# Moving the token differences of two of the four difference products of the w_out matmul from GpSimd to VectorE, with new contention constants in the ordering

## The chip, the cores and the metric

The kernel runs on one core of one Trainium2 chip. The metric is the device time of one execution in microseconds (us), lower is better; several runs are given by their median.

## What is computed

Attention in chunks of 64 tokens, then a relu-squared feed-forward layer, then a gated feed-forward layer, all in float32 (the reference, cut):

```python
scores = scale * np.matmul(q_c, k_c.transpose(0, 1, 2, 4, 3))   # 8 batches, 8 heads, 9 chunks of 64, head size 64
attn = softmax(scores)
x = (attn @ v_c) as tokens                   # 4608 tokens x 512
h = np.maximum(x @ w_in, 0.0)                # w_in 512 x 2048
y = h * h @ w_out                            # w_out 2048 x 512
gate = 1.0 / (1.0 + np.exp(-(y @ w_gate)))   # w_gate, w_val 512 x 1536
out = gate * (y @ w_val) @ w_out2            # w_out2 1536 x 512
```

## The kernel before, in words

All features lie on the 128 partitions, tokens on the free axis. Every large matmul is made by a Strassen-like scheme: the two operands are cut in 2 x 2 blocks, and seven products P1 to P7 take the place of eight. Four of them (P5, P6, P7, P4) take a difference of two token blocks as their moving operand, the other three (P1, P2, P3) a block as it is. Every operand is split in two fp32r parts, high and low: ScalarE rounds it (line 428), VectorE subtracts the rounded part from it (`split`, line 433), and TensorE adds up three fp32r matmuls for each (high x high, low x high, high x low).

The w_out product is made by class `Long` (from line 898), one object for each of six pairs of token blocks of 384 tokens. The inner size of 2048 is 16 blocks of 128: eight for each half, so each product has eight groups (index `kp`) of six matmuls of 128x384 (two output halves by three terms, line 934). `long_units` (line 986) gives the products' order on TensorE: P1 of this pair, P4 of the last pair, then P2, P5, P6, P3, P7 of this pair. `blocks_g` (line 1097) loads the blocks g of h*h from DRAM with a look of 13 us; b11, b12 and b22 are loaded once in a pair, b21 twice. `Long.product` calls `minus` (line 905) ahead of the four difference products, and `minus` issues eight subtractions of 128x384 through `binary` (line 439), here on GpSimd for all four: 4 x 8 x 6 = 192 in this stage. They are made in place: P5 turns b11 into b12 - b11, P6 turns that into b22 less it, P7 turns b12 into b22 - b12, P4 subtracts from the second b21 what P6 left. Then `split(x, r, n, look=5.0)` (line 927) makes the operand; the `look` of 5.0 lets the planner take its buffer at most 5 us before the split is due. The last stage (the gated layer's w_out2) uses `Long` too, with blocks of 512.

The order of all instructions on all engines comes from a planner (class `Plan`, from line 52). Each piece of work is a job with an engine, a planned cost and the buffers that it reads and writes. `due` (line 89) works backward from TensorE's order to a due time for each job; `run` (line 119) simulates all engines and lets each engine take, when it is free, the ready job with the earliest due time that its memory allows. Costs come from `cost` (line 397), as fixed part plus part per element, and jobs marked `shared` (VectorE's and GpSimd's work with all operands in SBUF) are lengthened when the other engine is at a shared job (lines 203 to 206). The times of this simulation set only the order; on the chip each engine runs its list and waits on semaphores. The weights of the gated layer are prepared beside the w_out stage (`weight_group`, line 526, buffers `wf`, `ws`, `wx`): conversions on ScalarE and VectorE, an integer addition and four sums on GpSimd, splits, and a DMA to DRAM.

Of the kernel before, what the change touches and what calls it, by code (L numbers as in the profile page):

```python
# [14 lines left out]
ALU = mybir.AluOpType  # L15
# [36 lines left out]
class Plan:  # L52
# [66 lines left out]
    def run(self):  # L119
# [4 lines left out]
        engines = {e: 0.0 for e in ("PE", "ACT", "DVE", "POOL", "SP")}  # L124
# [9 lines left out]
                heapq.heappush(ready[j.eng], (j.due, j.n))  # L134
        events, order = [], []
        t, dma, shift, done = 0.0, 0.0, 0.0, 0
        port = {"DVE": 0.0, "POOL": 0.0}
        stall, why = 0.0, {}

        def place(b):  # L140
# [50 lines left out]
        def begin(j):  # L191
            nonlocal dma, done, shift
            j.start, j.started = t, True
            done += 1
            order.append(j)
            if j.eng == "SP":
                engines["SP"] = t + j.cost
                dma = max(dma, t) + j.bytes / 270e3
                j.end = max(dma, t + j.cost) + self.DMA_LATENCY
            else:  # L200

                cost = j.cost
                if j.shared:
                    other = "POOL" if j.eng == "DVE" else "DVE"
                    cost += min(cost, max(0.0, port[other] - t)) * (1.0 if j.eng == "DVE" else 0.4)
                    port[j.eng] = t + cost
                engines[j.eng] = t + cost
                j.end = t + cost + (0.35 if j.eng == "PE" else 0.15)
            heapq.heappush(events, (engines[j.eng], ~j.n))
            heapq.heappush(events, (j.end, j.n))  # L210
# [3 lines left out]
        while done < len(jobs):  # L214
            moved = True
            while moved:
                moved = False
                for e in engines:
# [23 lines left out]
                    while ready[e] and tries < 600:  # L242
                        due, n = heapq.heappop(ready[e])
                        j = jobs[n]
# [31 lines left out]
            t, n = heapq.heappop(events)  # L276
# [3 lines left out]
            for n in batch:  # L280

                j = jobs[n if n >= 0 else ~n]
# [41 lines left out]
def tile_attention_relu2_glu(  # L324
# [24 lines left out]
    BL1 = 384  # L349
# [45 lines left out]
        return Buf(psum=True, name=name)  # L395

    def cost(eng, n, flat=None):
        per = {"ACT": (0.17, 0.0009), "DVE": (0.1, 0.00115), "POOL": (0.2, 0.0022)}[eng]
        return per[0] + per[1] * n


# [37 lines left out]
    def binary(eng, o, a, b, op, n, ob, ib, soon=None, look=None):  # L439
        e = {"DVE": nc.vector, "POOL": nc.gpsimd}[eng]  # L440
        return job(
            eng, cost(eng, n), lambda: e.tensor_tensor(out=o(), in0=a(), in1=b(), op=op),  # L442
            [*ib], [*ob], soon=soon, look=look, shared=not any(x.psum for x in ib),
        )
# [165 lines left out]
    def product(ps, ops, xs, p, n, first, cost_of, at_=None):  # L610
        kind, half = A_OF[p]
        op, x = ops[kind], xs[B_OF[p]]
        size = op.size // 8
        reads = [op, *x]

        def go():
            o = at(ps, n)
            for kk in range(2):
                if len(x) == 2:
                    xb, off, xsize = x[kk], 0, n  # L620
                else:
                    xb, off, xsize = x[0], kk * n, 2 * n
                for i, (wi, xi) in enumerate(((0, 0), (1, 0), (0, 1))):
                    nc.tensor.matmul(  # L624
                        out=o,
                        lhsT=at(op, P, F32R, wi * size + half * HB + kk * P),
                        rhs=at(xb, n, F32R, xi * xsize + off),
                        start=(first and kk == 0 and i == 0),
                        stop=(kk == 1 and i == 2),
                        skip_group_check=True,  # L630
                    )

        return job("PE", 6 * cost_of, go, reads if first else [*reads, ps], [ps], stream="main", at=at_)
# [208 lines left out]
    class Unit:  # L842
        def __init__(self, ops, xs, n, per, finish, tag):
            self.ops, self.xs, self.n, self.per, self.finish, self.tag = ops, xs, n, per, finish, tag
# [51 lines left out]


    class Long:
        def __init__(self, ops, blocks, n, per, finish):
            self.ops, self.blocks, self.n, self.per, self.finish = ops, blocks, n, per, finish  # L900

        def words(self, b):
            return lambda: at(b, self.n)

        def minus(self, o, x, y):
            for oo, xx, yy in zip(o, x, y):
                binary("POOL", self.words(oo), self.words(xx), self.words(yy), ALU.subtract,
                       self.n, [oo], {oo, xx, yy})

        def product(self, ps, p, first):  # L910
            n = self.n
            need = {"P1": "11", "P2": "21", "P5": "11 12", "P6": "11 22", "P3": "22", "P7": "12 22", "P4": "11 21"}[p]
            have = {x: self.blocks((int(x[0]) - 1, int(x[1]) - 1)) for x in need.split()}
            b11, b12, b21, b22 = (have.get(x) for x in ("11", "12", "21", "22"))
            src = {"P1": b11, "P2": b21, "P5": b11, "P6": b11, "P3": b22, "P7": b12, "P4": b21}[p]
            if p == "P5":
                self.minus(b11, b12, b11)
            elif p == "P6":
                self.minus(b11, b22, b11)
            elif p == "P7":  # L920
                self.minus(b12, b22, b12)
            elif p == "P4":
                self.minus(b21, b21, b11)
            kind, half = A_OF[p]
            for kp, r in enumerate(src):
                x = Buf(8 * n, name="x", op=True)
                split(x, r, n, look=5.0)
                w = self.ops[kp][kind]

                def go(kp=kp, x=x, w=w):  # L930
                    size = w.size // 8
                    for m in range(2):
                        for i, (wi, xi) in enumerate(((0, 0), (1, 0), (0, 1))):
                            nc.tensor.matmul(  # L934
                                out=at(ps[m], n),
                                lhsT=at(w, P, F32R, wi * size + half * HB + m * P),
                                rhs=at(x, n, F32R, xi * n),
                                start=(first and kp == 0 and i == 0),
                                stop=(kp == len(src) - 1 and i == 2),
                                skip_group_check=True,  # L940
                            )

                new = first and kp == 0
                job("PE", 6 * self.per, go, [w, x] if new else [w, x, *ps], ps, stream="main")
# [65 lines left out]
    with tc.manual_schedule():  # L1010

        per1, per, per_h = 0.1735, 0.227, 0.1195
        pairs1 = NT // (2 * BL1)
# [83 lines left out]
        def blocks_g(s):  # L1097
            def load(r, c):
                got = []
                for kp in range(G1):  # L1100
                    t = sbuf(BL1, "g")
                    f, b = r * G1 + kp, 2 * s + c
                    dma(lambda t=t: at(t), lambda f=f, b=b: gd[f][:, b * BL1:(b + 1) * BL1],
                        [gb[f, b]], [t], size=P * BL1 * 4, look=13.0)
                    got.append(t)
                return got

            return block_loader(load)

        def finish_y(s):  # L1110
            def finish(u, m, col, t):
                a = (2 * s + col) * BL1
                d = yb[m, 2 * s + col] = Buf(name="yd")
                dma(lambda: yd[:, m, a:a + BL1], lambda: at(t), [t], [d], size=P * BL1 * 4, soon=3.0)
            return finish

        def y_of(m, a, n):
            return [yb[m, b] for b in range(a // BL1, (a + n - 1) // BL1 + 1)]

        w1out = [weight_group(None, f, G1, f"wo{f}", True, look=55.0, raws=raws1, by=rows, have=w1f) for f in range(G1)]  # L1120
        long_units([
            (lambda s=s: Long(w1out, blocks_g(s), BL1, per1, finish_y(s))) for s in range(pairs1)
        ])


# [92 lines left out]
        def finish3(s):  # L1218
            def finish(u, m, col, t):
                n = u.n  # L1220
                o = sbuf(n, "o")
                job("DVE", 0.1 + 0.00118 * n, lambda: nc.vector.transpose(out=at(o), in_=at(t)), [t], [o], soon=2.0)
                t0 = s[col] * BLK if len(s) == 2 else col * HB

                def dst():
                    return [out[t0:t0 + n, m * P + 32 * g:m * P + 32 * g + 32].rearrange(
                        "(b t) c -> t b c", t=32) for g in range(4)]

                def src():
                    return [at(o)[32 * g:32 * g + 32].rearrange("p (b c) -> p b c", c=32) for g in range(4)]  # L1230

                dma(dst, src, [o], size=P * n * 8, n=4, soon=2.0)
            return finish

        long_units([
            (lambda s=s: Long(wo, last_blocks(s), BLK if len(s) == 2 else HB,
                              per if len(s) == 2 else per_h, finish3(s)))
            for s in order[1]
        ])

# [31 lines left out]
```

## Time and profile before

| | |
|---|---|
| median of 3 runs | 1705.0 us (1704.69 to 1706.76) |
| profiled execution | 1700.49 us |
| its span, first to last instruction | 1698.7 us |
| mean granted TensorE clock | 0.990 |
| busy: TensorE, VectorE, ScalarE, GpSimd | 1632.5, 1419.0, 985.7, 953.9 us |
| stages by the trace: start-up; attention and w_in; w_out; gate and value; w_out2 | to 150; 520.5; 895.5; 1431.6; 1698.7 us |

In the profile PE is TensorE's matmuls, PEld its weight loads, DVE VectorE, ACT ScalarE, POOL GpSimd, SP the queue that issues the DMAs. Times are us from the span's start. A busy time counts each instruction from its start to its end; overlapping instructions of TensorE are counted once. L934 is line 934 of the kernel. The share of busy time is an average over stages; what bounds a stage is read from that stage.

### The profile page before, as it was taken

What the parts mean: (1) busy time and instruction counts of PE and PEld (TensorE: products, weight loads), DVE (VectorE), ACT (ScalarE), POOL (GpSimd) and SP (SyncE); (2) the same over time, 40 slices, a digit from 0 to 9 for tenths busy, and PEclk for the clock granted to TensorE, in tenths of its full rate; (3) what the DMA queues carried; (4) which work ended last, traced back from release to release, by engine and by line L of the source; (5) the groups of instructions that cost most, each with busy time, mean ns of one, the idle gap of its engine ahead of it and who ended that gap; (6) DMA issues with size and microseconds to landing.
All of it is one profiled execution on the core that took longest, in us unless ns stands there. A gap on an engine that the chain in (4) does not pass through costs nothing. (4 is left out here: it accounts for less than half of the span.)

```text
span 1698.7 us, 30837 instructions
## 1 busy us (share of the span) xinstructions
PE 1632.5 (96%) x10452; PEld 1453.1 (86%) x10452; DVE 1419.0 (84%) x1928; ACT 985.7 (58%) x1974; POOL 953.9 (56%) x740
## 2 busy tenths in 40 slices
PE   6789999999999999999999999999999999999998
PEld 5678999899999998999988879878887789788888
DVE  7998686768789999999999988764678855999996
ACT  7676565666676555655556656544545644455554
POOL 2653021211358678768687777653656745777662
PEclk8999999999999999999999999999999999999999
DMA  9925657676686644854885853687365478666662
GB/s 246 217 80 156 160 139 197 175 207 180 206 285 203 199 164 131 276 177 131 270 301 171 289 182 137 223 286 259 131 217 217 158 274 300 194 166 162 169 169 50
DMA packets 390798, 333.35 MB, mean 196 GB/s; under 512 B 234736, under 2 KB 325616, under 8 KB 390640
## 3 DMA queue, kind: packets, MB, share of 16 engines
q1 hardware_dynamic: 390640, 331.38, 63.0%
q8 instruction: 82, 1.34, 0.3%
q14 instruction: 76, 0.62, 0.1%
HBM read 209.13 MB, written 122.16 MB: 195 GB/s over the span
## 5 line engine op out<-in xcount | busy, mean ns | idle before, releaser
L498 POOL TENSOR_TENSOR wf__2712<-wf__2712,wr__2649 128x512 int32<-128x512 int32 x16 | 20.9, 1305 | 229.5 <-DVE wf__2712 L491 131.1
L442 POOL TENSOR_TENSOR raw__537<-raw__696,raw__537 128x384 f32<-128x384 f32 x24 | 30.0, 1268 | 41.7 <-DVE B__730 L433 24.7
L498 POOL TENSOR_TENSOR wf__6803<-wf__6803,wr__6481 128x512 int32<-128x512 int32 x18 | 26.9, 1495 | 45.7 <-DVE wf__6803 L491 36.6
L498 POOL TENSOR_TENSOR wf__7393<-wf__7393,wr__6481 128x512 int32<-128x512 int32 x18 | 25.1, 1397 | 38.8 <-DVE wf__7393 L491 19.5
L479 ACT ACTIVATE wr__6481<-wr__6481 128x512 int32<-128x512 uint32 x36 | 23.9, 664 | 0.0
L433 DVE TENSOR_TENSOR wx__8063<-ws__7534,wx__8063 128x512 fp32r<-128x512 f32 x18 | 20.5, 1141 | 1.3 <-ACT wx__8063 L428 1.3
L475 ACT ACTIVATE wf__6803<-wr__6481 128x512 f32<-128x512 f32 x18 | 12.0, 664 | 15.2 <-DVE wx__8063 L433 8.3
L482 DVE TENSOR_SCALAR wf__7393<-wf__7393 128x512 f32<-128x512 f32 x18 | 13.2, 731 | 8.6 <-ACT wf__7393 L475 8.6
L433 DVE TENSOR_TENSOR wx__7334<-ws__7534,wx__7334 128x512 fp32r<-128x512 f32 x18 | 16.4, 912 | 3.7 <-ACT wx__7334 L428 3.7
L442 DVE TENSOR_TENSOR b__10264<-b__10264,bank 128x512 f32<-128x512 f32 x7 | 4.8, 688 | 16.8 <-PE bank L624 12.1
L482 DVE TENSOR_SCALAR wf__6803<-wf__6803 128x512 f32<-128x512 f32 x18 | 11.8, 656 | 7.7 <-ACT wf__6803 L475 7.7
L498 POOL TENSOR_TENSOR w__669<-w__669,wraw__374 128x512 int32<-128x512 int32 x1 | 1.3, 1289 | 29.7 <-DVE w__669 L491 29.7
L442 DVE TENSOR_TENSOR b__10691<-b__10691,bank 128x512 f32<-128x512 f32 x7 | 4.8, 686 | 15.2 <-PE bank L624 13.3
L442 POOL TENSOR_TENSOR ws__7534<-wf__6803,wf__7393 128x256 f32<-128x256 f32 x18 | 17.1, 952 | 0.5
L442 POOL TENSOR_TENSOR ws__7534<-ws__7534,wf__6803 128x256 f32<-128x256 f32 x18 | 16.7, 926 | 1.0
L433 DVE TENSOR_TENSOR wx__7443<-wf__7393,wx__7443 128x256 fp32r<-128x256 f32 x18 | 15.2, 842 | 1.6 <-ACT wx__7443 L428 1.6
L491 DVE SCALAR_TENSOR_TENSOR wf__7393<-wr__6481,wf__7393 128x512 int32<-128x512 int32 x18 | 16.1, 894 | 0.3
L491 DVE SCALAR_TENSOR_TENSOR wf__6803<-wr__6481,wf__6803 128x512 int32<-128x512 int32 x18 | 15.6, 866 | 0.3
L484 DVE TENSOR_SCALAR wf__7393<-wf__7393 128x512 int32<-128x512 int32 x18 | 15.2, 843 | 0.6
L442 POOL TENSOR_TENSOR raw__696<-raw__696 128x384 f32<-128x384 f32 x12 | 14.8, 1249 | 0.0
L475 ACT ACTIVATE wf__7393<-wr__6481 128x512 f32<-128x512 f32 x18 | 11.9, 664 | 4.6 <-DMA wr__6481<-in_moe_w_val_dram 2.2
L442 POOL TENSOR_TENSOR raw__537<-raw__537 128x384 f32<-128x384 f32 x12 | 14.5, 1226 | 0.0
(5638 smaller groups left out, 6671.8 us busy)
## 6 DMA issues: line engine op xcount, KB each, us to landing
ad<-wx__7334 SPq DMA_DIRECT2D x27, 512.0 KB, 4.5
ad<-wx__8063 SPq DMA_DIRECT2D x27, 512.0 KB, 4.2
wr__2649<-in_moe_w_out_dram SPq DMA_DIRECT2D x16, 512.0 KB, 4.5
wr__6481<-in_moe_w_gate_dram SPq DMA_DIRECT2D x12, 512.0 KB, 4.5
wr__6481<-in_moe_w_val_dram SPq DMA_DIRECT2D x12, 512.0 KB, 4.2
wr__6481<-in_moe_w_out_dram SPq DMA_DIRECT2D x12, 512.0 KB, 3.9
ad<-wx__7443 SPq DMA_DIRECT2D x18, 256.0 KB, 3.7
wf<-wf__2712 SPq DMA_DIRECT2D x16, 256.0 KB, 4.7
```

What stands on the lines that cost most here:

```text
L433: lambda: nc.vector.tensor_tensor(out=lo(), in0=at(src, n, F32, off), in1=hi().bitcast(F32), op=ALU.subtract),
L442: eng, cost(eng, n), lambda: e.tensor_tensor(out=o(), in0=a(), in1=b(), op=op),
L475: nc.scalar.activation(out=at(w), in_=t[:, :, 1].bitcast(F32), func=ACTF.Abs)
L479: nc.scalar.activation(out=low, in_=low.bitcast(U32), func=ACTF.Copy, scale=2.0**-29)
L482: nc.vector.tensor_scalar_max(at(w), at(w), TINY)
L484: nc.vector.tensor_scalar(out=wi, in0=wi, scalar1=5, scalar2=2, op0=ALU.logical_shift_left, op1=ALU.logical_shift_right,)
L491: nc.vector.scalar_tensor_tensor(out=wi, in0=words()[:, :, 1], scalar=-0x40000000, in1=wi, op0=ALU.bitwise_and, op1=ALU.bitwise_or,)
L498: nc.gpsimd.tensor_tensor(out=wi, in0=wi, in1=words()[:, :, 0], op=ALU.add)
```

## The change

The subtractions of P5 and P6 of the w_out product go to VectorE, those of P7 and P4 stay on GpSimd. The last stage's `Long` gets an empty table, so all four stay on GpSimd there. The planner's cost of a GpSimd instruction becomes 0.3 + 0.0024 n. Its contention rule changes: a VectorE job that starts while GpSimd is at a shared job is lengthened by 0.45 of GpSimd's remaining time, at most 0.82 of its own cost, and by a debt that GpSimd jobs ran up when they started beside a VectorE job; a GpSimd job is lengthened by 0.1 of the overlap instead of 0.4. The rule holds for all stages.

```diff
-        port = {"DVE": 0.0, "POOL": 0.0}
+        port = {"DVE": 0.0, "POOL": 0.0, "debt": 0.0}
...
-                if j.shared:
-                    other = "POOL" if j.eng == "DVE" else "DVE"
-                    cost += min(cost, max(0.0, port[other] - t)) * (1.0 if j.eng == "DVE" else 0.4)
-                    port[j.eng] = t + cost
+                if j.shared and j.eng == "DVE":
+                    cost += port["debt"] + min(0.82 * cost, 0.45 * max(0.0, port["POOL"] - t))
+                    port["debt"], port["DVE"] = 0.0, t + cost
+                elif j.shared:
+                    cost += 0.1 * min(cost, max(0.0, port["DVE"] - t))
+                    port["debt"] += 0.45 * min(cost, max(0.0, port["DVE"] - t))
+                    port["POOL"] = t + cost
...
-        per = {"ACT": (0.17, 0.0009), "DVE": (0.1, 0.00115), "POOL": (0.2, 0.0022)}[eng]
+        per = {"ACT": (0.17, 0.0009), "DVE": (0.1, 0.00115), "POOL": (0.3, 0.0024)}[eng]
...
     class Long:
-        def __init__(self, ops, blocks, n, per, finish):
+        def __init__(self, ops, blocks, n, per, finish, engines):
+            self.engines = engines
...
-        def minus(self, o, x, y):
+        def minus(self, p, o, x, y):
             for oo, xx, yy in zip(o, x, y):
-                binary("POOL", self.words(oo), self.words(xx), self.words(yy), ALU.subtract,
+                binary(self.engines.get(p, "POOL"), self.words(oo), self.words(xx), self.words(yy), ALU.subtract,
                        self.n, [oo], {oo, xx, yy})
...
-            (lambda s=s: Long(w1out, blocks_g(s), BL1, per1, finish_y(s))) for s in range(pairs1)
+            (lambda s=s: Long(w1out, blocks_g(s), BL1, per1, finish_y(s), {"P5": "DVE", "P6": "DVE"})) for s in range(pairs1)
...
-                              per if len(s) == 2 else per_h, finish3(s)))
+                              per if len(s) == 2 else per_h, finish3(s), {}))
```

## Rows read from the trace of the kernel before

**Rows 1.** The page's first part: busy time, share of the span and instructions by engine.

```profile
PE 1632.5 (96%) x10452; PEld 1453.1 (86%) x10452; DVE 1419.0 (84%) x1928; ACT 985.7 (58%) x1974; POOL 953.9 (56%) x740
```

**Rows 2.** Busy time by stage: stretch, its length, each engine's busy us, clock, DMA.

```profile
0.00:150.00 150.00, 117.12 (x1309) 103.30 (x1310) 134.75 (x216) 105.78 (x219) 74.07 (x70) 0.92 0.74 180
150.00:520.50 370.50, 363.22 (x3349) 341.60 (x3348) 284.27 (x518) 238.68 (x524) 89.54 (x80) 1.00 0.68 196
520.50:895.50 375.00, 366.83 (x2019) 348.65 (x2018) 368.62 (x427) 214.64 (x440) 283.00 (x226) 1.00 0.60 198
895.50:1431.60 536.10, 525.02 (x2521) 440.80 (x2520) 384.92 (x494) 293.38 (x550) 331.77 (x249) 0.99 0.63 223
1431.60:1698.70 267.10, 260.32 (x1260) 218.79 (x1259) 246.45 (x277) 133.18 (x244) 175.54 (x119) 1.00 0.57 148
```

**Rows 3.** Line 934 in the w_out stage, then TensorE's timeline at both its ends.

```profile
520.50:895.50 375.00, 366.71 (x2016) 348.31 (x2016) 1.00 0.60 198
...
520.56 1.20 PE L934 MATMUL bank<-x__6303,woa__5763 128*128 128x384 f32 x6
521.60 1.20 PE L934 MATMUL bank<-x__6330,woa__5793 128*128 128x384 f32 x6
...
895.27 0.86 PE L624 MATMUL bank<-B__9769,g__9480 128*128 128x512 f32 x3
```

**Rows 4.** Busy time by products: P2, P5, P6 of each pair; last, the final stretch.

```profile
528.88:556.59 27.71, 27.25 (x146) 24.61 (x145) 27.14 (x27) 16.54 (x37) 23.32 (x19) 1.00 0.25 78
590.13:616.88 26.75, 26.71 (x146) 24.68 (x146) 26.75 (x30) 13.80 (x28) 22.38 (x18) 1.00 0.23 74
651.43:679.70 28.27, 26.59 (x145) 24.73 (x145) 28.27 (x32) 14.21 (x29) 21.34 (x18) 1.00 0.33 105
712.98:740.90 27.92, 27.50 (x145) 24.59 (x145) 27.92 (x30) 15.01 (x31) 23.11 (x19) 1.00 0.31 101
774.18:802.21 28.03, 27.89 (x145) 24.52 (x145) 28.00 (x27) 13.15 (x27) 26.13 (x21) 1.00 0.27 86
835.74:864.63 28.89, 27.52 (x146) 24.47 (x145) 28.86 (x30) 15.13 (x32) 25.72 (x21) 1.00 0.92 318
...
864.63:895.44 30.81, 27.27 (x146) 26.42 (x146) 30.66 (x36) 18.23 (x35) 23.25 (x18) 0.94 0.66 226
```

**Rows 5.** GpSimd's timeline in the second pair: four of a run of 24 differences.

```profile
581.22 1.02 POOL L442 TENSOR_TENSOR g__6342<-g__6424,g__6342 128x384 f32<-128x384 f32 x1 [5.69 <-DMA g__6424<-gd]
...
602.73 1.01 POOL L442 TENSOR_TENSOR g__6247<-g__6396,g__6247 128x384 f32<-128x384 f32 x1
...
608.84 1.32 POOL L442 TENSOR_TENSOR g__6823<-g__6195,g__6823 128x384 f32<-128x384 f32 x1
610.12 1.32 POOL L442 TENSOR_TENSOR g__6842<-g__6220,g__6842 128x384 f32<-128x384 f32 x1
```

**Rows 6.** VectorE's timeline before and during that run: splits (L433), a PSUM addition.

```profile
575.97 0.54 DVE L433 TENSOR_TENSOR x__6399<-g__6301,x__6399 128x384 fp32r<-128x384 f32 x1
576.44 0.54 DVE L433 TENSOR_TENSOR x__6468<-g__6815,x__6468 128x384 fp32r<-128x384 f32 x1
...
588.89 1.37 DVE L433 TENSOR_TENSOR x__6427<-g__6478,x__6427 128x384 fp32r<-128x384 f32 x1
590.19 1.37 DVE L433 TENSOR_TENSOR x__6303<-g__6195,x__6303 128x384 fp32r<-128x384 f32 x1
...
601.80 0.54 DVE L442 TENSOR_TENSOR e__2080<-e__2080,bank 128x384 f32<-128x384 f32 x1
```

**Rows 7.** TensorE at the run's end; its weight loads' largest wait on VectorE.

```profile
605.01 1.44 PE L934 MATMUL bank<-x__6399,wos__6394 128*128 128x384 f32 x6
606.29 1.45 PE L934 MATMUL bank<-x__6468,wos__6476 128*128 128x384 f32 x6
...
PEld bank L934 <- DVE x__6383 L433: 3.3, 9, 0.8
```

**Rows 8.** Line 442 in the w_out stage: VectorE's and GpSimd's busy time and instructions.

```profile
520.50:895.50 375.00, 18.12 (x36) 269.81 (x218) 1.00 0.60 198
```

More of the change, by code (lines that the diff above doesn't have):

```diff
@@ L916, in product @@
             if p == "P5":
-                self.minus(b11, b12, b11)
+                self.minus(p, b11, b12, b11)
             elif p == "P6":
-                self.minus(b11, b22, b11)
+                self.minus(p, b11, b22, b11)
             elif p == "P7":
-                self.minus(b12, b22, b12)
+                self.minus(p, b12, b22, b12)
             elif p == "P4":
-                self.minus(b21, b21, b11)
+                self.minus(p, b21, b21, b11)
             kind, half = A_OF[p]
```

## The prediction

> **What bounds the kernel now.** First the page's busy line [rows 1]: TensorE is busy 96% of the span and VectorE 84%, but these are averages over stages with different limits. So next the busy time by stage [rows 2]. In the w_out stage, from 520.5 to 895.5 us, VectorE is busy 368.62 of 375.00 us (98.3%), GpSimd 283.00, TensorE 366.83. In no other stage do both elementwise engines come so near to full at once.
>
> A busy TensorE is not TensorE at its peak, so I count its pace. Its 2016 matmuls of line 934 are 336 groups of six (one token block each); a free group starts 1.04 us after the one before, the first at 520.56, and the next stage's first matmul follows at 895.27 [rows 3]. At the free pace 336 groups take 336 x 1.04 = 349.4 us; they took 374.7. **The excess is 25.3 us**, and that is the most that this stage can give.
>
> Where it lies: the six stretches of the products P2, P5, P6 (24 groups, 24.96 us free) last 167.6 us together instead of 149.8, so 17.8 us of it is theirs. The last stretch (P3, P7 and P4 of the last pair, also 24 groups) lasts 30.81 instead of 24.96: 5.9 us, at the hand-over to the next stage, where granted clock dips to 0.94 [rows 4]. The remaining products hold 1.7.
>
> Why P5 and P6: GpSimd makes the differences of P5, P6 and P7 of one token pair as one unbroken run of 24, from 581.22 to 611.4 us, one each 1.28 us; the single one that ran beside VectorE's PSUM additions took 1.01 [rows 5]. Beside such a run VectorE makes one split per GpSimd instruction: starts 1.30 us apart, 1.37 long. With GpSimd still, the same split takes 0.54 and the next starts 0.47 later; the PSUM addition keeps 0.54 in the middle of the run [rows 6]. So the two engines go in lockstep at 1.29 us a pair, and **each GpSimd difference costs VectorE 1.29 - 0.47 = 0.82 us**. TensorE wants a split each 1.04 us, so in such a run VectorE loses 0.25 us per group; 24 of them eat 6 us, more than the lead of about 5 us that the splits' look of 5.0 allows. At the end of the run TensorE's groups come 1.28 apart, and its weight loads wait for VectorE's split [rows 7]. Four runs of eight per pair, six pairs: 192 differences, of line 442's 218 on GpSimd [rows 8].
>
> **The change, part by part.** *Removed from GpSimd:* the differences of P5 and P6, 2 x 8 x 6 = 96, at 1.29 us: 124 us of its 283 in this stage. GpSimd is on nobody's path by itself, so this alone gives nothing. What it gives is VectorE's time: 96 x 0.82 = 78.7 us.
>
> *Added to VectorE:* 96 subtractions of 128x384 f32 with both inputs in SBUF. That is the split's own form, so the price lies between 0.47 us (GpSimd still) and 1.29 us (in lockstep) [rows 6]. I take 0.47, since of the unbroken run of 24 only eight stay, and the differences can be made before or after those: 96 x 0.47 = 45.1 us. VectorE's load: 368.6 - 78.7 + 45.1 = 335.0 us, for TensorE's 349.4. At 1.29 each it would be 413.8, and the stage slower; both ends are used below.
>
> By the Trainium skill (SBUF — State Buffer, Who interferes with whom) the shared port pair is an exclusive lock for a whole instruction whenever VectorE has two SBUF inputs and GpSimd reads SBUF; a pair would then take 1.01 + 0.47 = 1.48 us, a difference would cost VectorE 1.01, and the load would fall to 316.8. The trace has 1.29, and it decides; nothing below uses the 1.48.
>
> *What a P5 or P6 product then needs:* a difference and a split per group, 0.94 us on VectorE against TensorE's 1.04. It keeps up, barely. The P7 run of eight that is left costs 8 x 0.25 = 2 us of the lead of 5, and the P4 run the same in another place. So the 17.8 us of P2, P5 and P6 can go nearly to nothing; bounds 0 and 17.8. I leave 2.8 (half a microsecond per pair, for weight work of the GLU stage that falls between): **15 us gained**. The 5.9 at the hand-over stay: there GpSimd turns to the GLU stage's token differences, which are not moved. The 1.7 stay too.
>
> *Waits that move:* each moved difference waits on VectorE for the load of its second block. Behind it on that engine stand the splits, for which TensorE waits. GpSimd waited 5.69 us so at the start of one run, idle and early [rows 5]; an equally late load on VectorE would use up the lead, so its price is 0 to about 1 us per pair. I take 0: that run starts at 581.22 [rows 5], and TensorE reaches its product at 590.13 + 8 x 1.04 = 598.5 at the earliest [rows 4], 17 us later. No DMA is added or removed, no instruction moves to SP, and ScalarE's copies for the splits are the same.
>
> *The planner's constants:* a GpSimd instruction is now planned at 0.3 + 0.0024 n instead of 0.2 + 0.0022 n (1.22 us for 384, nearer to the 1.29 of the trace than 1.04), and the mutual delays are charged otherwise. For a run of eight both versions charge VectorE some 0.6 us per GpSimd instruction, so I expect no drift in one direction. But every stage's order is drawn anew. TensorE's idle time outside this stage is 32.9 us in the first 150 us, and 11.1 and 6.8 in the last two stages [rows 2]; the stage between has 7.3. I take 0 and keep plus and minus 6 us, a tenth of those 58.
>
> **Sum.** The profiled execution took 1700.5 us around a span of 1698.7; minus 15 is 1685.5. The median of the runs shown is 1705.0, 4.5 above it, and all terms are differences, so I forecast 1705 - 15 = **1690 us**. A change of less than 0.2% (3.4 us) can't be told from none here.
>
> **The rivals.** *Same: the stall finds another place.* P6's differences and P7's need the same blocks (b22), so GpSimd's run for P7 starts just when VectorE has P6's to make. Beside that run of 10.3 us VectorE makes eight instructions while TensorE uses up ten groups; if all eight are differences rather than splits, the lead shrinks by 10 us and TensorE stalls 5 us per pair, against 25.3 / 6 = 4.2 now. Against it: VectorE's order goes by due time, and splits that are due first go first; with three or fewer differences among the eight the lead holds (5 us, less the 2 us above, is three groups). Time: about 1704. Chance 0.14.
>
> *Slower: VectorE is the full engine and gets more to do.* GpSimd's freed 124 us are filled with preparation of the GLU weights, whose additions of SBUF words stretch VectorE just as the differences did. VectorE's relief per microsecond of GpSimd work that vanishes is 0.82 / 1.29 = 0.64, so the 45.1 us added are paid for as long as 71 us stay empty: the point is a refill of 53 us, where GpSimd's work other than differences is now 283 - 192 x 1.29 = 35 us in this stage. At 88 us of refill VectorE gets 45.1 - 0.64 x 36 = 22 us more, and the GLU stage, thus relieved, can give back at most its 11.1: some 12 us slower, 1717. For it: VectorE has no idle time to show for [rows 2], and the planner fills what is ready. Against it: weight work has far later due times and needs VectorE itself between its GpSimd steps. Chance 0.12.
> The Trainium skill (Perfetto Trace Analysis, Optimizing Scalar/DVE Operations) points the same way: a saturated VectorE should hand work to ScalarE or even GpSimd; but it adds that between these two it might not help, as they share a port, and the lockstep of this trace agrees with that half.
>
> *Faster still:* the whole 25 goes, since the hand-over also gets an earlier GpSimd: 1680. Chance 0.10. *Lost elsewhere:* the 15 us come, and the new order loses as much in the first 150 us or the GLU stage: 1702 to 1708. Chance 0.06. The forecast has the other 0.58. That the subtraction would not run on VectorE is excluded: the engine is an argument of the call.
>
> **How the numbers follow.** Faster by over 0.2%: 0.58 and 0.10, and 0.04 from the rival of the other place, which may keep a few microseconds: 0.72. Same: the rest of that rival and half of the loss elsewhere: 0.13. Slower: the refill and what is left: 0.15. The forecast's own range is 1683 to 1697 (15 gained, plus or minus 6, and 1 for the wait). With the 25 us case below and the cases near zero above it becomes 1679 to 1707; the refill is left out.
>
> **What would show it.** In the changed trace: the w_out stage in about 360 us; 96 differences on GpSimd, in runs of eight; P5 and P6 groups 1.04 apart; VectorE's subtraction at 0.47 apart outside the runs and 1.29 inside; VectorE's share still above 93%. Wrong if P6's groups still come 1.28 apart, if runs of weight work fill GpSimd to 88 us beside its differences, or if the first 150 us or the GLU stage moves by over 6 us.

## The result and the profile after

The changed kernel takes 1680.82 us (median of four runs, 1678.82 to 1681.26), beside 1705.51 for the kernel before: a ratio of 0.9852, 95% interval 0.9835 to 0.9869. That is 24.7 us faster, where 15 were forecast. The profiled execution took 1678.82 us around a span of 1677.0, 21.7 us less than the span of before.

The page's busy line, the answer to [rows 1]:

```profile
PE 1623.2 (97%) x10452; PEld 1458.9 (87%) x10452; DVE 1397.7 (83%) x2024; ACT 981.9 (59%) x1974; POOL 836.7 (50%) x644
```

96 instructions have gone from GpSimd to VectorE, and yet VectorE's busy time is lower than before (1397.7, was 1419.0). Next the busy time by stage, the answer to [rows 2]; the stages are cut at each stage's first matmul (and at 150 us):

```profile
0.00:150.00 150.00, 116.70 (x1280) 103.36 (x1281) 130.86 (x210) 101.72 (x211) 66.41 (x64) 0.90 0.75 180
150.00:527.05 377.05, 369.37 (x3378) 349.51 (x3377) 287.16 (x523) 240.86 (x529) 91.82 (x82) 0.99 0.67 193
527.05:881.75 354.70, 352.06 (x2017) 349.03 (x2017) 345.82 (x530) 217.11 (x445) 170.80 (x135) 1.00 0.67 221
881.75:1423.20 541.45, 538.22 (x2589) 451.08 (x2589) 398.73 (x501) 298.92 (x561) 341.05 (x252) 1.00 0.62 219
1423.20:1677.00 253.80, 246.87 (x1194) 205.87 (x1192) 235.12 (x265) 123.33 (x231) 166.63 (x113) 1.00 0.56 145
```

The last cut lies 15 us late: the w_out2 stage's first matmul starts at 1407.88. With it the stages are 527.1 (was 520.6), **354.7 (374.7)**, **526.1 (536.1)** and 269.2 us (267.3): 6.5 us lost ahead of the w_out product, 20.0 gained in it, 10.0 gained in the gate and value stage (the GLU stage below), 1.9 lost in the last.

The busy time by products, the answer to [rows 4], P2, P5 and P6 of each pair and then the final stretch:

```profile
535.37:560.88 25.51, 25.49 (x146) 24.84 (x145) 25.51 (x42) 14.40 (x34) 10.14 (x8) 1.00 0.21 73
594.16:619.12 24.96, 24.96 (x146) 24.96 (x145) 24.05 (x37) 14.63 (x30) 11.06 (x9) 1.00 0.33 104
652.40:677.36 24.96, 24.96 (x146) 24.96 (x145) 24.93 (x41) 13.98 (x30) 10.29 (x8) 1.00 0.34 111
710.64:736.68 26.04, 25.49 (x145) 24.89 (x145) 25.46 (x42) 14.87 (x32) 10.10 (x8) 1.00 0.32 109
769.96:794.92 24.96, 24.96 (x145) 24.96 (x145) 24.33 (x41) 14.61 (x31) 10.01 (x8) 1.00 0.35 116
828.20:853.38 25.18, 25.18 (x145) 24.94 (x145) 24.77 (x42) 14.18 (x31) 11.93 (x8) 1.00 1.00 366
853.38:881.75 28.37, 26.30 (x145) 24.76 (x145) 28.34 (x33) 17.85 (x35) 23.80 (x18) 1.00 0.84 297
```

At the free pace of 1.04 us a group each row would be 24.96. Three of the six are exactly that; the six sum to 151.6 us, an excess of 1.9 (it was 17.8). GpSimd's busy time in each has gone from over 21 us to between 10 and 12. The final stretch, which is the hand-over to the next stage, has 3.4 us of excess. Before it was 5.7: [rows 4] cuts that stretch at 895.44, but the next stage's first matmul starts at 895.27 [rows 3]. What is left of the stage, 168 groups, takes 174.7 us, which is 168 x 1.04: no excess. The total excess is 5.3 us, was 25.3.

VectorE's timeline in the second pair, the answer to [rows 6]: L446 with g is a moved difference, L437 a split.

```profile
589.37 0.55 DVE L446 TENSOR_TENSOR g__6753<-g__6322,g__6753 128x384 f32<-128x384 f32 x1
589.84 0.55 DVE L446 TENSOR_TENSOR g__6491<-g__7010,g__6491 128x384 f32<-128x384 f32 x1
590.30 0.55 DVE L437 TENSOR_TENSOR x__7053<-g__6160,x__7053 128x384 fp32r<-128x384 f32 x1
...
597.56 1.36 DVE L437 TENSOR_TENSOR x__6305<-g__6737,x__6305 128x384 fp32r<-128x384 f32 x1
598.84 1.37 DVE L437 TENSOR_TENSOR x__7053<-g__6426,x__7053 128x384 fp32r<-128x384 f32 x1
...
608.22 0.55 DVE L446 TENSOR_TENSOR g__6753<-g__6294,g__6753 128x384 f32<-128x384 f32 x1
608.68 0.55 DVE L437 TENSOR_TENSOR x__6975<-g__6426,x__6975 128x384 fp32r<-128x384 f32 x1
```

And GpSimd's run for P7 in between, first and last of eight, the answer to [rows 5]:

```profile
592.61 1.92 POOL L446 TENSOR_TENSOR g__6972<-g__7055,g__6972 128x384 f32<-128x384 f32 x1 [14.24 <-DMA g__7055<-gd]
...
602.34 1.33 POOL L446 TENSOR_TENSOR g__7044<-g__6202,g__7044 128x384 f32<-128x384 f32 x1
```

P5's differences come before the run, and instructions start 0.47 us apart there; only the last two of the eight overlap the run's first difference, and are no longer for it. In the run VectorE makes splits alone, in lockstep at 1.29; P6's differences come after it, alternating with splits, again at 0.47.

Not every pair is so clean. In the last pair, VectorE and then GpSimd:

```profile
834.00 1.37 DVE L437 TENSOR_TENSOR x__7553<-g__6322,x__7553 128x384 fp32r<-128x384 f32 x1
835.29 1.36 DVE L446 TENSOR_TENSOR g__6972<-g__8651,g__6972 128x384 f32<-128x384 f32 x1
836.57 1.37 DVE L437 TENSOR_TENSOR x__9520<-g__6270,x__9520 128x384 fp32r<-128x384 f32 x1
837.87 1.37 DVE L446 TENSOR_TENSOR g__6426<-g__6327,g__6426 128x384 f32<-128x384 f32 x1
```

```profile
832.16 2.79 POOL L446 TENSOR_TENSOR g__6839<-g__7532,g__6839 128x384 f32<-128x384 f32 x1 [8.15 <-DMA g__7532<-gd]
834.91 1.33 POOL L446 TENSOR_TENSOR g__7044<-g__6258,g__7044 128x384 f32<-128x384 f32 x1
```

Here four of the sixteen moved differences go in lockstep with GpSimd's run. In the whole stage it is 12 of 96, at 1.36 to 1.38 us each; the other 84 take 0.54 to 0.56.

### The profile page after: what moved, and what is told of

It reads as the page before. It is cut to its first block, busy times and chain, and to the rows that moved or that the text cites. A ratio compares the mean times of both kernels' runs of the same rounds, so it can differ in the third digit from the quotient of the medians.

```text
span 1677.0 us, 30764 instructions
## 1 busy us (share of the span) xinstructions
PE 1623.2 (97%) x10452; PEld 1458.9 (87%) x10452; DVE 1397.7 (83%) x2024; ACT 981.9 (59%) x1974; POOL 836.7 (50%) x644
## 5 line engine op out<-in xcount | busy, mean ns | idle before, releaser
L446 POOL TENSOR_TENSOR raw__537<-raw__696,raw__537 128x384 f32<-128x384 f32 x24 | 28.7, 1211 | 59.8 <-DVE B__706 L437 26.5
L437 DVE TENSOR_TENSOR wx__7302<-ws__7507,wx__7302 128x512 fp32r<-128x512 f32 x18 | 18.6, 1032 | 4.2 <-ACT wx__7302 L432 4.2
L437 DVE TENSOR_TENSOR wx__7676<-ws__7507,wx__7676 128x512 fp32r<-128x512 f32 x18 | 17.7, 986 | 4.5 <-ACT wx__7676 L432 4.3
L446 POOL TENSOR_TENSOR ws__7507<-wf__6816,wf__7364 128x256 f32<-128x256 f32 x18 | 17.2, 956 | 0.4
L446 POOL TENSOR_TENSOR ws__7507<-ws__7507,wf__6816 128x256 f32<-128x256 f32 x18 | 16.1, 897 | 1.3
L437 DVE TENSOR_TENSOR wx__7419<-wf__7364,wx__7419 128x256 fp32r<-128x256 f32 x18 | 16.4, 909 | 0.0
L446 POOL TENSOR_TENSOR raw__537<-raw__537 128x384 f32<-128x384 f32 x12 | 15.1, 1275 | 0.0
L486 DVE TENSOR_SCALAR wf__7364<-wf__7364 128x512 f32<-128x512 f32 x18 | 10.6, 590 | 5.3 <-ACT wf__7364 L479 5.3
L495 DVE SCALAR_TENSOR_TENSOR wf__7364<-wr__6450,wf__7364 128x512 int32<-128x512 int32 x18 | 14.7, 818 | 0.1
L446 POOL TENSOR_TENSOR raw__696<-raw__696 128x384 f32<-128x384 f32 x12 | 14.6, 1235 | 0.0
L417 ACT ACTIVATE c__1728<-c__1728 128x384 f32<-128x384 f32 x20 | 10.4, 520 | 6.3 <-DVE c__1728 L446 6.2
L486 DVE TENSOR_SCALAR wf__6816<-wf__6816 128x512 f32<-128x512 f32 x18 | 9.0, 502 | 6.0 <-ACT wf__6816 L479 6.0
L837 ACT ACTIVATE raw__537<-bank 128x256 f32<-128x256 f32 x36 | 12.1, 381 | 2.0 <-DVE T__973 L437 1.3
```

Source lines behind the costliest of these rows:

```text
L417: lambda: nc.scalar.activation(out=o(), in_=i(), func=func, **kw), ib, ob, soon=soon,
L437: lambda: nc.vector.tensor_tensor(out=lo(), in0=at(src, n, F32, off), in1=hi().bitcast(F32), op=ALU.subtract),
L486: nc.vector.tensor_scalar_max(at(w), at(w), TINY)
L495: nc.vector.scalar_tensor_tensor(out=wi, in0=words()[:, :, 1], scalar=-0x40000000, in1=wi, op0=ALU.bitwise_and, op1=ALU.bitwise_or,)
L837: nc.scalar.activation(out=o[:, :, a:a + CH], in_=i, func=ACTF.Copy)
```

## The experiments

All were run on one chip per group, each group beside its own runs of the kernel before (medians 1703.26, 1701.30 and 1701.81 us). "Blocks" counts the integer additions on GpSimd that prepare a block of GLU weights (36 in all) and that are done when that stage begins. Stage times are from one trace of each kernel.

| | ratio (95% interval) | first | w_out | GLU | last | blocks |
|---|---|---|---|---|---|---|
| before | 1 | 520.6 | 374.7 | 536.1 | 267.3 | 8 |
| changed | 0.9852 (0.9835 to 0.9869) | 527.1 | 354.7 | 526.1 | 269.2 | 10 |
| E1 move alone | 0.9856 (0.9840 to 0.9872) | 524.1 | 352.5 | 533.5 | 268.9 | 10 |
| E2 planner alone | 1.0054 (1.0035 to 1.0074) | 525.2 | 378.6 | 539.9 | 269.3 | 7 |
| E3 before, short differences | 0.9875 (0.9856 to 0.9895) | 524.0 | 355.0 | 536.1 | 267.3 | 8 |
| E4 changed, short differences | 0.9840 (0.9819 to 0.9861) | 529.6 | 352.5 | 526.0 | 269.3 | 10 |
| E5 all four, new planner | 0.9923 (0.9905 to 0.9941) | 527.8 | 350.0 | 541.7 | 269.3 | 8 |
| E7 all four, old planner | 0.9919 (0.9903 to 0.9934) | 521.1 | 349.9 | 545.7 | 267.8 | 8 |
| E8 P7 alone, old planner | 1.1004 (1.0982 to 1.1027) | 519.0 | 359.3 | 720.9 | 268.0 | 8 |
| E9 P4 alone, old planner | 1.0111 (1.0092 to 1.0131) | 520.4 | 369.1 | 558.5 | 267.2 | 6 |
| E10 longer look | 0.9887 (0.9871 to 0.9903) | 524.7 | 362.8 | 524.3 | 265.9 | 11 |
| E11 shorter look | 0.9945 (0.9928 to 0.9963) | 528.6 | 356.0 | 540.7 | 267.8 | 7 |
| E12 all four, longer look | 0.9894 (0.9878 to 0.9910) | 527.5 | 350.0 | 537.9 | 268.5 | 8 |
| E13 three | 0.9886 (0.9870 to 0.9903) | 522.1 | 351.9 | 535.7 | 269.1 | 8 |

**E1 and E2: the move and the planner apart.** E1 keeps the new `engines` table and takes back the planner:

```diff
-                if j.shared and j.eng == "DVE":
-                    cost += port["debt"] + min(0.82 * cost, 0.45 * max(0.0, port["POOL"] - t))
...
+                if j.shared:
+                    other = "POOL" if j.eng == "DVE" else "DVE"
+                    cost += min(cost, max(0.0, port[other] - t)) * (1.0 if j.eng == "DVE" else 0.4)
...
-        per = {"ACT": (0.17, 0.0009), "DVE": (0.1, 0.00115), "POOL": (0.3, 0.0024)}[eng]
+        per = {"ACT": (0.17, 0.0009), "DVE": (0.1, 0.00115), "POOL": (0.2, 0.0022)}[eng]
```

> The differences of P5 and P6 on VectorE, the planner's constants and contention rule as before the change. Lockstep theory (each GpSimd difference costs VectorE 0.82 us, the move takes half of them away): the w_out stage falls from 374.7 to about 355 us as in the changed kernel, the first stage keeps its 520.5 us, the total is about 1680 to 1690 us. Ordering theory (the new constants order the work better, the move itself is worth little): the w_out stage stays above 368 us, the total above 1697.

E2 is the reverse:

```diff
-            (lambda s=s: Long(w1out, blocks_g(s), BL1, per1, finish_y(s), {"P5": "DVE", "P6": "DVE"})) for s in range(pairs1)
+            (lambda s=s: Long(w1out, blocks_g(s), BL1, per1, finish_y(s), {})) for s in range(pairs1)
```

> The planner's new constants and contention rule alone; all four kinds of differences stay on GpSimd. Lockstep theory: the w_out stage stays at 368 to 378 us, since VectorE still loses 0.82 us to each of 192 differences; the first stage takes 527 us as in the changed kernel; total 1700 to 1712. Ordering theory: the w_out stage falls to 355 to 362 us and the GLU stage by up to 10, total 1680 to 1690.

The w_out stage of E1, then that of E2 (columns as in [rows 2]):

```profile
524.11:876.60 352.49, 350.68 (x2018) 349.24 (x2017) 342.94 (x526) 217.01 (x440) 162.11 (x131) 1.00 0.67 223
```

```profile
525.15:903.78 378.63, 368.06 (x2017) 348.32 (x2017) 366.44 (x421) 211.16 (x435) 283.94 (x223) 1.00 0.58 187
```

E1 took 1678.64 us, a little below what was expected; its ratio is that of the changed kernel, though its first stage took 524.1 us where 520.5 was expected. E2 took 1712.54, half a microsecond above the bound that was expected of the lockstep theory, and its GLU stage went the other way from the changed kernel's. So the ordering theory fell: the constants and the rule alone make the kernel slower by 0.54%, and beside the move they are worth nothing in total. They seem to cost about 5 us ahead of the w_out product: the first stage of six traces with the old constants takes 519.0 to 524.1 us, mean 521.5, of eight with the new ones 522.1 to 529.6, mean 526.6.

**E3: less GpSimd time, nothing else.** In the kernel before, in its own order, this leaves out 352 of the 384 columns of each difference of P5 and P6 (the diff is cut):

```diff
-        def minus(self, o, x, y):
-            for oo, xx, yy in zip(o, x, y):
-                binary("POOL", self.words(oo), self.words(xx), self.words(yy), ALU.subtract,
+        def minus(self, o, x, y, m=None):
+            def words(z):
+                return lambda: at(z, m or self.n)
+
+            for oo, xx, yy in zip(o, x, y):
+                binary("POOL", words(oo), words(xx), words(yy), ALU.subtract,
...
-                self.minus(b11, b12, b11)
+                self.minus(b11, b12, b11, 32 if self.n == BL1 else None)
...
-                self.minus(b11, b22, b11)
+                self.minus(b11, b22, b11, 32 if self.n == BL1 else None)
```

> The kernel before in its own order and on its own engines, but the GpSimd differences of P5 and P6 in the w_out stage compute 32 of 384 columns (the rest of those operands is left undifferenced). Nothing is added to VectorE, and every wait between GpSimd, ScalarE and VectorE is still there. Lockstep theory: what counts is how long GpSimd holds VectorE up, so the w_out stage falls to 353 to 358 us and the total to about 1682 to 1690. Rival (the gain comes from waits between the engines that vanish when VectorE makes the difference itself): the stage stays above 368 us.

Its w_out stage, and the GLU stage behind it:

```profile
524.01:879.03 355.02, 351.15 (x2018) 350.86 (x2018) 299.82 (x427) 220.06 (x440) 196.36 (x225) 1.00 0.64 209
879.03:1415.13 536.10, 525.04 (x2521) 440.85 (x2521) 386.46 (x494) 293.25 (x550) 330.16 (x249) 0.99 0.63 223
```

This is the cleanest of the runs: the same instructions on the same engines in the same order, and the stage falls by 19.7 us. VectorE makes the same instructions as before in 299.8 us instead of 368.6 [rows 2], while GpSimd's time falls from 283.0 to 196.4: 68.8 us of VectorE for 86.6 of GpSimd, 0.79 for each. In P2, P5 and P6 no excess is left. The rival of vanished waits fell, and lateness of GpSimd's differences can't make up the 19.7 us either: in the kernel before, all of VectorE's waits in this stage come to 5.6 us, and TensorE waits for ScalarE for 3.8. And the GLU stage, which the edit does not touch, takes 536.1 us in both.

**E4: the price on VectorE.** In the changed kernel:

```diff
+            def words(z):
+                return lambda: at(z, 32 if p in self.engines else self.n)
+
             for oo, xx, yy in zip(o, x, y):
-                binary(self.engines.get(p, "POOL"), self.words(oo), self.words(xx), self.words(yy), ALU.subtract,
+                binary(self.engines.get(p, "POOL"), words(oo), words(xx), words(yy), ALU.subtract,
```

> The changed kernel in its own order, but the differences of P5 and P6 on VectorE compute 32 of 384 columns (the rest is left undifferenced), which takes off VectorE about 0.35 us for each of 96 instructions, 33 us in the w_out stage. If the 45 us that the change adds to VectorE are hidden beside TensorE: the same time, 1677 to 1683 us, w_out stage 352 to 355. If VectorE is still the bound of the stage (345.8 of 354.7 us busy): the stage comes to 350 us and the total falls by 4 to 5 us.

```profile
529.55:882.00 352.45, 350.80 (x2018) 349.27 (x2017) 312.51 (x530) 218.81 (x445) 165.92 (x135) 1.00 0.67 223
```

VectorE is relieved of 33.3 us (345.8 to 312.5), as worked out, and the stage falls by 2.2 (one trace each), to the lower end of what "hidden" said. So of these 33 us some nine tenths are covered by TensorE's work; 2.2 us are not.

**E5 and E7: all four on VectorE**, with the new and the old planner.

```diff
-{"P5": "DVE", "P6": "DVE"}
+{"P5": "DVE", "P6": "DVE", "P7": "DVE", "P4": "DVE"}
```

> All four kinds of differences of the w_out product on VectorE, the new planner constants. Lockstep theory: VectorE's busy time in the stage falls once more, by 96 x 0.35 = 34 us, but TensorE already goes at its free pace, so the stage can only lose what is left of its excess: 350 to 355 us against 354.7, total 1672 to 1684 us. Rival (VectorE saturated, each further instruction on it costs 0.47 us): the stage gets 30 us or more longer than in the changed kernel.

> All four kinds of differences on VectorE, the planner's constants and rule as before the change. As for the same move with the new constants: stage 350 to 355 us, total 1672 to 1684. If the new constants are worth something once both engines have less to do together, this one is slower than that by over 4 us.

E5's w_out and GLU stages:

```profile
527.79:877.74 349.95, 349.69 (x2018) 349.39 (x2018) 327.18 (x615) 217.59 (x435) 39.41 (x33) 1.00 0.64 210
877.74:1419.43 541.69, 525.39 (x2521) 439.94 (x2521) 390.77 (x501) 295.94 (x558) 329.78 (x248) 0.99 0.62 219
```

The stage itself came as expected, at 350.0 and 349.9 us, TensorE's free pace to within 0.6. VectorE carries 192 more instructions than in the kernel before and is busy 41 us less. But the total missed (1672 to 1684 was expected): 1687.97 and 1687.44, because the GLU stage takes 541.7 and 545.7. Old and new constants differ by less than a microsecond in total.

**E8 and E9: one product alone**, old planner; both take 48 differences off GpSimd.

```diff
-{"P5": "DVE", "P6": "DVE"}
+{"P7": "DVE"}      # E8
+{"P4": "DVE"}      # E9
```

> Only the differences of P7 (48) on VectorE, planner constants as before the change. Run theory (what stalls TensorE is a run of GpSimd differences so long that the splits' lead of about 5 us is used up; 0.25 us lost in each group): the run of 24 becomes one of 16, which takes 4 us of the lead, so the stage falls to 354 to 360 us. Load theory (only VectorE's total load counts; 48 differences take 48 x 0.35 = 17 us off it, half of what the change takes off): the stage falls by about half of the change's 20, to 362 to 367 us.

> Only the differences of P4 (48) on VectorE, planner constants as before the change. Run theory: the run of 24 for P5, P6 and P7 stays, and with it most of the stall: stage 366 to 374 us. Load theory: as for P7 alone, 362 to 367 us.

E8's w_out stage and the longest wait of its GLU stage; then E9's w_out and GLU stages:

```profile
518.98:878.24 359.26, 354.00 (x2017) 350.50 (x2017) 351.32 (x476) 214.10 (x439) 233.32 (x177) 1.00 0.63 208
...
PE bank L625 <- DMA v__11084<-ad: 189.3, 1, 189.3
```

```profile
520.40:889.48 369.08, 362.33 (x2017) 347.18 (x2017) 343.53 (x458) 210.84 (x425) 212.36 (x167) 1.00 0.59 187
889.48:1448.01 558.53, 533.67 (x2521) 442.70 (x2521) 400.68 (x511) 301.71 (x565) 343.20 (x259) 0.98 0.63 223
```

In the w_out stage the run theory holds and the load theory falls: with P7 moved and the run of 24 cut to 16 the stage takes 359.3, with P4 moved and the run of 24 left it takes 369.1, though VectorE is less busy there (343.5 us of 369.1, against 351.3 of 359.3). In P2, P5 and P6 the excess is 2.8 us in E8 and 14.7 in E9 (17.8 before). The traces have the runs: with pauses under 1 us GpSimd's longest is 15 differences in E8, and 24 in E9 and in the kernel before. Both totals are slower than before all the same, and for a reason outside that stage: in E8 TensorE stands still for 189 us in the GLU stage until a weight comes back from DRAM; the drawn order puts 24 of the 28 remaining blocks' additions (970 to 1145 us) ahead of that load.

**E10 to E12: how early the weights may be prepared.**

```diff
-        LK = 260.0, 500.0
+        LK = 320.0, 560.0     # E10 (two differences), E12 (all four)
+        LK = 150.0, 390.0     # E11 (two differences)
```

> The changed kernel, with the planner allowed to begin the preparation of the GLU weights 60 us earlier (looks of 320 and 560 instead of 260 and 500). Preparation theory (the GLU stage is the shorter, the more of the 36 weight blocks are prepared when it begins: 10 in the changed kernel, 8 in the kernel before, 6 with P4 alone): more than 10 blocks at its begin, GLU stage 520 to 526 us against 526.1, w_out stage 352 to 360, total 1675 to 1682. Rival (the GLU stage's length comes out of each new order by chance): no relation to the count.

> The changed kernel, with the preparation of the GLU weights allowed 110 us later (looks of 150 and 390). Preparation theory: it cannot begin before about 720 us, so at most 6 blocks are ready when the GLU stage begins; that stage takes 545 us or more, the w_out stage 350 to 354 since less weight work runs beside it, total 1693 to 1710. Rival (chance): the GLU stage stays within 522 to 540.

> All four kinds of differences on VectorE, new planner constants, looks of 320 and 560. Preparation theory: the four-fold move lost 15 us in the GLU stage because only 8 blocks were ready; with a longer look 9 or more are, so the GLU stage falls from 541.7 to 525 to 536 us, the w_out stage stays at 350 to 352, total 1668 to 1683. If VectorE has no room for more weight work beside four kinds of differences, the count stays 8 and the GLU stage at 540 or more.

The integer additions in the w_out stage of the kernel before, of the changed kernel, of E10 (one more lies just ahead of it) and of E11, each with GpSimd's busy time:

```profile
520.50:895.30 374.80, 13.33 (x8) 1.00 0.60 199
```

```profile
527.05:881.75 354.70, 15.80 (x10) 1.00 0.67 221
```

```profile
524.73:887.57 362.84, 17.29 (x10) 0.99 0.65 217
```

```profile
528.60:884.59 355.99, 10.07 (x7) 1.00 0.62 202
```

E10 has 11 blocks ready and a GLU stage of 524.3 us, as expected, but its w_out stage rises to 362.8, out of the range: 6.0 us of its excess of 13.4 lie in P5 and P6 of the first pair and 6.1 in the last stretch. That the earlier weight work pushes it there is likely, but was not tried by itself. What one stage gains the other pays. E11 has 7 blocks, one more than I thought possible (its first addition comes at 677 us, not 720), and a GLU stage of 540.7: longer than the changed kernel's by 14.6, short of the 545 that was expected and just beyond the rival's 540. Its w_out stage missed too, at 356.0 where 350 to 354 was expected. E12 keeps 8 blocks at 537.9 us: between its two expectations, and no faster than the changed kernel (1683.33).

**E13: three on VectorE**, P4 left on GpSimd.

```diff
-{"P5": "DVE", "P6": "DVE"}
+{"P5": "DVE", "P6": "DVE", "P7": "DVE"}
```

> The differences of P5, P6 and P7 on VectorE, those of P4 on GpSimd, new planner constants. Run theory: one run of eight is left per pair, no stall: w_out stage 350 to 353 us. Preparation theory: the total goes by the blocks that are ready at 880 us: with 8 or fewer the GLU stage takes 535 to 546 and the total 1682 to 1692; with 10 it takes 526 to 534 and the total 1672 to 1680.

```profile
522.10:873.95 351.85, 349.68 (x2017) 349.39 (x2017) 334.64 (x571) 218.01 (x439) 99.90 (x82) 1.00 0.64 212
873.95:1409.65 535.70, 524.18 (x2521) 438.32 (x2521) 394.49 (x496) 293.78 (x554) 332.79 (x249) 1.00 0.62 221
```

Both stages came as expected: 351.9, and with 8 blocks 535.7; the total of 1681.81 is 0.2 us below its range. Over all orders the GLU stage goes with the blocks: 6 blocks 558.5 us; 7 blocks 539.9 and 540.7; 8 blocks 535.7 to 545.7 (six kernels, E8 left aside); 10 blocks 526.0 to 533.5; 11 blocks 524.3. It is a trend with a scatter of up to 10 us, and each of these kernels has an order of its own (but for E3 and E4), so the count alone is not shown to be the cause.

No version beats the changed kernel clearly. The best stages seen, 519 + 350 + 524 + 266 us, come to 1659, but in no single order.

## Why the prediction was right, and where its sum fell short

The direction and the mechanism held. The size did so only in part: 1680.82 us lies outside the forecast's own 1683 to 1697, inside 1679 to 1707 thanks to the rival "faster still", whose 1680 it meets without that rival's whole 25 us in this stage. And one sign of being wrong came true: the GLU stage moved by 10 us, where over 6 was to count.

**Lockstep, 0.82 us of VectorE per GpSimd difference:** E3 shows it by itself, with 0.79 us of VectorE per microsecond of GpSimd taken away where 0.64 was worked out; cutting a difference to 32 columns gave VectorE 68.8 / 96 = 0.72 us, with the short instruction still there. **The run, not the load:** shown by E8 against E9, and by E5, where 192 more instructions on VectorE leave it less busy and TensorE at its free pace. The unbroken run of 24 was read off one pair; the other five pairs have it in pieces, with pauses of 0.2 to 3.4 us. That VectorE's load must fall below TensorE's 349.4 us was not what mattered: in E9 it is 343.5, and the excess is 19.6.

**0.47 us for a moved difference:** right for 84 of them. The 12 in lockstep cost 1.29, so the 96 take 55.7 us of VectorE (each counted to its end or to the next start) and not 45.1. That is nearly all of why its load is 345.8 us and not 335.0: the splits gave back 76.8 us, near the 78.7 forecast, and the GLU weights take 29.8 us of VectorE, as before (29.7). **The wait for a load on VectorE at nothing:** right; the largest one in the stage is 0.5 us. **Hidden:** of 33 us E4 finds all but 2.2 covered.

**The term that was mis-sized is the excess that stays.** I left 2.8 us in P2, P5 and P6, 5.9 at the hand-over and 1.7 elsewhere, 10.4 in all; measured are 1.9, 3.4 and 0.0, in all 5.3. So the stage gave 20 and not 15. The hand-over was called untouched; its excess of 5.7 falls by 2.3 us in the changed kernel and by 5.2 with all four moved. It stays at 5.6 in E3, at 5.7 in E8 and at 5.9 in E2, and is 2.1 in E1. So its relief seems to come with the move of P5 and P6 and not with the planner's constants; but E10, which has that move, is at 6.1, and by what step the relief comes was not tried.

**The second is "elsewhere 0".** The sum of the other stages did come near it (6.5 and 1.9 lost, 10.0 gained: 1.6 gained), but by luck, of large parts: the new constants seem to cost some 5 us ahead of the product, and the GLU stage gained 10 with two more weight blocks ready. E1 has the same count with the old constants and gains only 2.6 there, so that gain hangs on the drawn order and not on the move alone. Against the medians the gain was 24.7 us and not the 21.7 of the two profiled executions, since that of before was 5.0 us under its median of 1705.51 and this one 2.0. So of the 9.7 us that I missed the stage has 5.0, the other stages 1.6 and this 3.0.

*The rivals.* The stall did not find another place. In the second pair P6's differences wait until P7's run is over; in the last pair four moved differences stand in it, one more than the three that the prediction allowed, and still P2, P5 and P6 there lose only 0.2 us. The refill came to some 6 us of GpSimd's time (its work other than these differences went from 41 to 47), not to 53, and in that time two more weight blocks get ready. Of the Trainium skill's two sentences (Perfetto Trace Analysis, Optimizing Scalar/DVE Operations) the first says only that it may make sense to give away work of a saturated VectorE; here the reverse helped, and E5 shows it best, with a VectorE that was busy 98% relieved by more work. The second, that moving work between VectorE and GpSimd might not help, as they share a port, names a contention that the trace shows (1.29 us a pair), but in this direction the move did help, by 20 us in the stage.

## What to carry to other kernels

When two engines go in lockstep, price a move by the pair: here a GpSimd difference of 1.01 us cost VectorE 0.82, and the same difference on VectorE costs it 0.47 where it meets no GpSimd work, so the full engine gets emptier when work is moved onto it. Look for long unbroken runs on the off-path engine and compare what they take from the consumer's lead with that lead; a run cut by a third did more (E8) than the same number of instructions taken elsewhere (E9). Where one planner orders everything, measure each stage by itself: the stage that was changed obeyed its theory to a few microseconds, and the stages that were not changed moved by 10, twice by more: by 22 (E9) and by 185 (E8).

## What the runs showed of the hardware

The lockstep goes by the time that GpSimd's instructions take, not by their number: with its 32 columns a GpSimd difference takes 0.25 to 0.56 us in E3's second pair, and VectorE's splits beside these are mostly back at 0.55 to 0.61. It works the other way too: GpSimd's first difference of a run, starting while VectorE went from one such instruction to the next every 0.47 us, took 1.92 us in the second pair of the changed kernel and 2.79 in the last. TensorE keeps its free pace of 1.04 us a group, but for 5.3 us in all, beside a VectorE that is busy 97.5% of the stage. One order repeated gives the later stages to 0.1 us (GLU: 536.1 twice, 526.1 and 526.0; last: 267.3 and 267.2, 269.2 and 269.3), but the first stage moves by 2.5 to 3.4 us between two executions of one order, so much of the spread between runs may arise there.

That TensorE stood still in E8 shows in its granted clock, too: over these 190 us, in which TensorE was busy 3.93, it is 0.52, the lower of its two levels (1.2 GHz) nearly throughout.

```profile
960.00:1150.00 190.00, 3.93 (x18) 2.92 (x16) 81.99 (x131) 58.10 (x104) 76.87 (x77) 0.52 0.52 181
```
